# Row statistics of eight output tiles: running sums on ScalarE in place of bn_stats on VectorE, in an attention and spectral kernel

## The chip, the cores and the metric

The kernel runs on one core of one Trainium2 chip. The metric is the device time of one execution in microseconds (us). Before the change three runs gave 3757.16 us in the median (3756.23 to 3763.47). Differences are also given as a share of that.

A core has five engines with queues of their own: TensorE (PE, matmuls; its weight loads are listed as PEld), VectorE (DVE), ScalarE (ACT), GpSimd (POOL) and SyncE (SP, which issues DMA transfers). Each works through its own queue in order; semaphores make one wait for another.

## The reference

Two layers, each an attention block and a two-dimensional spectral filter, both with a layer norm in front and a residual. S is 2048 rows, D is 1024 columns, there are 32 heads of 32.

```python
def _A_ref(x, wqkv, wo):
    qkv = (x @ wqkv).reshape(B, S, 3, H, Dh).transpose(2, 0, 3, 1, 4)
    q, k, v = qkv[0], qkv[1], qkv[2]
    scores = jnp.einsum("bhqd,bhkd->bhqk", q, k) * (Dh ** -0.5)
    o = jnp.einsum("bhqk,bhkd->bhqd", _softmax(scores), v)
    return o.transpose(0, 2, 1, 3).reshape(B, S, D) @ wo

def _B_ref(x, w_r, w_i):
    X = jnp.fft.rfft2(x, axes=(-2, -1)) * (w_r + 1j * w_i)
    return jnp.fft.irfft2(X, s=(S, D), axes=(-2, -1))

for _ in range(2):
    x = x + _A_ref(_layernorm(x), wqkv, wo)
    x = x + _B_ref(_layernorm(x), w_r, w_i)
```

The change lies in the seam between the two: the output projection `@ wo` with its residual, and the mean and variance of every finished row, which the second layer norm needs.

## The kernel before

**Attention.** The heads are taken in 8 groups of four (`g`, 0 to 7). In a group, the queries are taken in 4 chunks of 512 (`c`) and the keys in 16 tiles of 128 (`kt`). One step (c, kt) is called a unit here; two units in a row make a slot, and a group has slots 0 to 31, eight to a chunk. For each unit `S` (line 703) lets TensorE form the scores of four heads in two PSUM tiles `s` from the pool psS, which has three buffers (L709), and ScalarE their exponentials `p` (L713). Every second unit, `PV` (L715) multiplies the last two units' `p` with the values (L719). `add` (L726) lets VectorE add `p` to two running sums `acc` in the tile R (L730, L732); these become the softmax's denominators. At a chunk's end, within the first unit of the next chunk, `fin` (L735) lets TensorE sum `acc` over the keys with a matrix of ones (L739, eight matmuls for four heads, into a psS tile `z`), and VectorE divides (L740 to L746). L739 therefore waits for the chunk's last add.

**The output projection.** It is spread over the loop as filler work for TensorE. A row tile has 128 rows and 1024 columns; tiles are numbered 0 to 15, four to a query chunk. `wo_parts` forms what the first seven head groups give to a tile (L538, with VectorE adding the residual at L564). The last head group's share can only be formed when that chunk's attention is done. So in group 7 `wo_rest(t)` (L598) finishes tile t: six matmuls of a psS tile (`wo_last`, L573, through L538; shown as s<-big,ohl), then L579 on VectorE, which scales, adds and so empties the psS buffer, then two `bn_stats` (L581), a store of the row tile to `y` (L582, from the SP queue) and a `bn_aggr` into `mvs` (L600), which holds mean and variance of tiles 0 to 11. Tiles 0 to 3 belong to chunk 0 and are finished in slots of chunk 1, and so on.

**What sets the order.** TensorE's and ScalarE's queues in the loop are in the order in which the code is written (`manual_schedule`). The table at L763 says in which slot of group 7 each tile is finished, and `share` (L762) how many filler matmuls follow in each slot. VectorE, GpSimd and SP are ordered by the scheduler.

**Behind the loop** `fold_rests` (L610) turns `mvs` into scales on GpSimd and normalises tiles 0 to 11 on ScalarE (L615), while TensorE forms tiles 12 to 15.

Of the kernel before, what the change touches and what calls it, by code (L numbers as in the profile page):

```python
# [6 lines left out]
F32 = mybir.dt.float32  # L7
# [4 lines left out]
AF = mybir.ActivationFunctionType  # L12
ALU = mybir.AluOpType
# [205 lines left out]
def run(g):  # L219
    for _ in g:  # L220
        pass
# [115 lines left out]
def attention(nc, tc, layer, ap, xin, yd, wts, wo, cst, dram, flags):  # L337
# [8 lines left out]
    sq, on, on2, sm = ap.sq, ap.on, ap.on2, ap.sm  # L346
# [14 lines left out]
    V, K, Q, bias, nrm, mx = {}, {}, {}, {}, {}, {}  # L361
# [15 lines left out]
    def turn_x(xn):  # L377
        p = psS.tile([128, 2, 512], F32, name="s").rearrange("p h (d n) -> p (h d) n", n=128)
        for d in range(8):
            nc.tensor.transpose(p[:, d], xn[:, 128 * d:128 * d + 128], cst["ident"])  # L380
        return p
# [107 lines left out]
    def sums(ph):  # L489
        return 8 if ph[0] == "v" else 4  # L490
# [41 lines left out]
    def wo_mm(p, c, t, n, ds, start=True, stop=True):  # L532

        for d in ds:
            oh, ol = ((olast[c][:, i] if d == 7 else osb[c][:, i, d])[:, t * 128:t * 128 + 128] for i in range(2))
            wh, wl = (wo_t[i][d // 4][:, d % 4, n * 512:n * 512 + 512] for i in range(2))
            for i, (a, b) in enumerate(((oh, wh), (oh, wl), (ol, wh))):
                nc.tensor.matmul(p, a, b, start=start and d == ds[0] and i == 0, stop=stop and d == ds[-1] and i == 2)  # L538
                yield
# [10 lines left out]
    mvs = sm.tile([128, 24], F32, name="mvs")  # L550
# [19 lines left out]
                    nc.vector.bn_aggr(mvs[:, 8 * c + 2 * t:8 * c + 2 * t + 2], st)  # L570
            yield

    def wo_last(c, t, p, src, y, start):  # L573

        for n in range(2):
            run(wo_mm(p[:, n], c, t, n, (7,), start=start))
        st = sm.tile([128, 2, 6], F32, name="st")
        r0 = c * 512 + t * 128
        nc.vector.scalar_tensor_tensor(y, p.rearrange("p n c -> p (n c)"), 1.0 / (SO * SW), src, op0=ALU.mult, op1=ALU.add)  # L579
        for n in range(2):  # L580
            nc.vector.bn_stats(st[:, n], y[:, n * 512:n * 512 + 512])  # L581
        nc.sync.dma_start(yd[r0:r0 + 128, :], y)  # L582
        return st

    wo_dst = [ap.x[:, 10 + t if t in SPILL else t] for t in range(8)] + [None] * 2 + [ap.x[:, t] for t in (10, 11)]
# [11 lines left out]

    def wo_rest(t):  # L598
        p = psS.tile([128, 2, 512], F32, name="s")
        nc.vector.bn_aggr(mvs[:, 2 * t:2 * t + 2], wo_last(t // 4, t % 4, p, wo_dst[t], wo_dst[t], True))  # L600

    def scale_bias(mv, n, m):

# [23 lines left out]
    with tc.manual_schedule(engines={mybir.EngineType.PE, mybir.EngineType.DVE, mybir.EngineType.Activation}):  # L627
# [14 lines left out]
        p = turn_x(xn)  # L642
# [13 lines left out]
        p = turn_x(xn)  # L656
# [4 lines left out]
        p = turn_x(xn)  # L661
# [5 lines left out]
        p = turn_x(xn)  # L667
# [35 lines left out]
    def S(g, c, kt):  # L703

        s = [psS.tile([128, 2, 512], F32, name="s") for _ in range(2)]
        for i, (a, b) in enumerate(((0, 0), (0, 1), (1, 0))):
            for h in range(4):
                r = slice(32 * h, 32 * h + 32)
                nc.tensor.matmul(s[h // 2][:, h % 2], K[g][r, a, kt * 128:kt * 128 + 128],  # L709
                                 Q[g][r, b, c * 512:c * 512 + 512], start=i == 0, stop=i == 2)  # L710
        for hf in range(2):
            p = P[g, c, kt, hf] = pp.tile([128, 2, 512], F32, name="p")
            nc.scalar.activation(p, s[hf], AF.Exp, bias=bias[g], scale=SCALE / (SQ * SQ))  # L713

    def PV(g, c, kt):  # L715
        if kt == 0:
            O[g, c] = psO.tile([128, 512], F32, name="o")
        for h in range(4):
            nc.tensor.matmul(O[g, c][32 * h:32 * h + 32], V[g][:, kt, 32 * h:32 * h + 32], P[g, c, kt, h // 2][:, h % 2],  # L719
                             start=kt == 0, stop=kt == NKT - 1)  # L720
        if kt == NKT - 1:
            o = ap.oc.tile([128, 512], F32, name="oc")
            nc.scalar.copy(o, O[g, c])
            O[g, c] = o

    def add(g, c, kt):  # L726
        for hf in range(2):
            p = P[g, c, kt, hf]
            if kt == 1:
                nc.vector.scalar_tensor_tensor(acc[hf], P[g, c, 0, hf], 1e-34, p, op0=ALU.add, op1=ALU.add)  # L730
            elif kt:
                last_add = nc.vector.tensor_add(acc[hf], acc[hf], p)  # L732
        return last_add if kt > 1 else None

    def fin(g, c):  # L735
        zt = on.tile([128, 16, 32], F32, name="zt")
        z = psS.tile([128, 2, 512], F32, name="s")[:, 0]
        for h in range(4):
            nc.tensor.matmul(z[32 * h:32 * h + 32], cst["ones"], acc[h // 2][:, h % 2], start=True, stop=True)  # L739
        nc.vector.transpose(zt.rearrange("p a b -> p (a b)"), z)  # L740
        rc = sm.tile([128, 16], F32, name="rc")
        nc.vector.reciprocal(rc, zt[:, :, 0])
        nc.vector.tensor_max(flags["r"], flags["r"], rc)
        r = on.tile([128, 512], F32, name="zt")
        nc.vector.transpose(r.rearrange("p (a b) -> p a b", b=32), rc.unsqueeze(2).broadcast_to([128, 16, 32]))
        nc.vector.scalar_tensor_tensor(r, O[g, c], SO, r, op0=ALU.mult, op1=ALU.mult)  # L746
        O[g, c] = r
# [12 lines left out]
    fill, lwo, wof = filler(), load_wo(), wo_parts()  # L760
    left, rests = 16, {}
    share = [21] * 10 + [7] * 6 + [11, 10] * 6 + [12] * 4  # L762
    for t, n in zip(range(11), (11, 12, 14, 15, 20, 22, 24, 26, 28, 29, 30)):  # L763
        rests[n] = t

    def slots(f, sums, n, steps):

        while sums:
            k = max(1, int(n / sums + 0.5))
            m = -(-steps // k)  # L770
            for i in range(0, steps, m):
                while ripe():
                    norms()
                for _ in range(min(m, steps - i)):
                    next(f, None)
                n -= 1
                yield sums - (i + m >= steps)
            sums -= 1

    with tc.manual_schedule(engines={mybir.EngineType.PE, mybir.EngineType.Activation}):  # L780
        for g in range(NG):
            todo = sum(sums(ph) for ph in beside.get(g, []))
            sl = slots(fill, todo, 22 if g == NG - 2 else 32, 24)
            wsl = slots(wof, 4, 10, 21)
            for u in range(NCH * NKT):
                c, kt = divmod(u, NKT)
                S(g, c, kt)
                if g == u == 0:
                    run(last_v)
                if kt % 2 == 0:  # L790
                    for w in pend:
                        PV(*w)
                    late = pend
                    pend = []
                    if kt == 0 and late:
                        for w in late:
                            last_add = add(*w)
                        with tc.issue_after(last_add.ins):
                            wts.look()
                        done = [late[1][:2]]  # L800
                        fin(*done[0])
                        late = []
                for w in late[:1]:
                    add(*w)
                late = late[1:]
                if kt == 5 and done:
                    out(*done.pop())
                pend.append((g, c, kt))
                if kt % 2 == 0:
                    continue  # L810
                if todo:
                    todo = next(sl)
                elif g == NG - 2:
                    if left:
                        run(lwo)
                        left = 0
                    if next(wsl, None) is not None and u == NCH * NKT - 1:
                        run(wsl)
                elif g == NG - 1:
                    if u // 2 in rests:  # L820
                        wo_rest(rests[u // 2])
                    for _ in range(share[u // 2]):
                        next(wof)
                if g == NG - 2 and todo <= 6 and left > (8 if todo > 4 else 0):
                    next(lwo)
                    left -= 1
        for w in pend:
            PV(*w)
        for w in late + pend:
            add(*w)  # L830
        run(wof)
    assert not wts.unseen and not wts.cols
    with tc.manual_schedule(engines={mybir.EngineType.PE}):
        ps, xs, folds = [], [xres(3, t) for t in range(4)], fold_rests()

# [557 lines left out]
```

## Time and profile before

| | us |
|---|---|
| median of three runs | 3757.16 |
| lowest, highest | 3756.23, 3763.47 |
| the profiled execution | 3758.82 |
| its span, first to last instruction | 3757.0 |

The profiled execution is a run of its own; its span is what the views cut up. A page of the profile gives busy time by engine, 40 slices, queues, the chain of work that ended last, and the costliest groups of instructions. Views of the trace give one engine's instructions in order of time, each with start, length, engine, line, operation, tile names and, in brackets, the idle time ahead of it and what ended that. Equal instructions in a row are merged, with their count behind an x. A view of stretches gives for each the busy time of every engine and the clock granted to TensorE (1.00 is full). Group 7 of layer 0 runs from about 1310 to 1580 us in the span, that of layer 1 from about 3180 to 3450 us. The costliest groups as the page has them (line, engine, operation, tiles, shapes, count; busy us, mean ns of one; idle time ahead of them and what ended most of it):

```profile
L713 ACT ACTIVATE p<-s,bias 128x1024 f32<-128x1024 f32 x2048 | 2171.5, 1112 | 555.6 <-PE s L709 537.6
L732 DVE TENSOR_TENSOR R<-R,p 128x1024 f32<-128x1024 f32 x1792 | 2088.1, 1218 | 126.1 <-ACT p L713 123.9
L719 PE MATMUL o<-p,R 128*32 128x512 f32 x8192 | 984.9, 598 | 0.0
```

### The profile page before, as it was taken

What the parts mean: (1) busy time and instruction counts of PE and PEld (TensorE: products, weight loads), DVE (VectorE), ACT (ScalarE), POOL (GpSimd) and SP (SyncE); (2) the same over time, 40 slices, a digit from 0 to 9 for tenths busy, and PEclk for the clock granted to TensorE, in tenths of its full rate; (3) what the DMA queues carried; (4) which work ended last, traced back from release to release, by engine and by line L of the source; (5) the groups of instructions that cost most, each with busy time, mean ns of one, the idle gap of its engine ahead of it and who ended that gap; (6) DMA issues with size and microseconds to landing.
All of it is one profiled execution on the core that took longest, in us unless ns stands there. A gap on an engine that the chain in (4) does not pass through costs nothing.

```text
span 3757.0 us, 80258 instructions
## 1 busy us (share of the span) xinstructions
PE 3688.9 (98%) x33271; PEld 1635.1 (44%) x33271; DVE 3212.6 (86%) x3874; ACT 2900.2 (77%) x3587; POOL 297.8 (8%) x388
## 2 busy tenths in 40 slices
PE   8999999999999999999999999999999999999998
PEld 5333433343343333378963334334433433333788
DVE  7799899989999988975658998999899999789745
ACT  5788888888888866658748888888888888666686
POOL 1000000000000000014410000000000000000243
PEclk9999999999999999999999999999999999999999
DMA  6000000000000211233250000001000102121423
GB/s 194 10 18 18 13 12 18 27 7 18 13 27 16 88 54 65 74 146 104 70 158 21 29 29 24 32 24 35 14 29 29 41 18 82 54 71 68 167 87 108
DMA packets 150120, 198.43 MB, mean 53 GB/s; under 512 B 58225, under 2 KB 104049, under 8 KB 148721
## 3 DMA queue, kind: packets, MB, share of 16 engines
q1 hardware_dynamic: 148416, 192.62, 15.9%
q8 instruction: 263, 4.31, 0.5%
q14 instruction: 113, 0.92, 0.1%
q10 hardware_dynamic: 1328, 0.59, 0.1%
HBM read 132.35 MB, written 48.23 MB: 48 GB/s over the span
## 4 chain that ended last, share of the span: by engine, by line


## 5 line engine op out<-in xcount | busy, mean ns | idle before, releaser
L713 ACT ACTIVATE p<-s,bias 128x1024 f32<-128x1024 f32 x2048 | 2171.5, 1112 | 555.6 <-PE s L709 537.6
L732 DVE TENSOR_TENSOR R<-R,p 128x1024 f32<-128x1024 f32 x1792 | 2088.1, 1218 | 126.1 <-ACT p L713 123.9
L719 PE MATMUL o<-p,R 128*32 128x512 f32 x8192 | 984.9, 598 | 0.0
L420 PE MATMUL x<-big,wqk 128*128 128x512 f16 x2880 | 676.4, 380 | 5.0 <-DVE Q L216 1.9
L709 PEld LDWEIGHTS <-R 32*128 32x128 f16 x12288 | 228.3, 92 | 739.7 <-issue 623.6
L420 PEld LDWEIGHTS <-wqk 128*128 128x128 f16 x3072 | 275.9, 98 | 421.7 <-issue 131.7
L719 PEld LDWEIGHTS o<-p,R 128*32 128x32 f32 x8192 | 213.7, 109 | 523.5 <-issue 523.5
L709 PE MATMUL s<-R 32*128 32x512 f16 x6144 | 425.7, 378 | 0.2
L709 PE MATMUL s<-Q,R 32*128 32x512 f16 x6144 | 425.7, 378 | 0.0
L477 PE MATMUL x<-wv,big 128*128 128x256 f16 x2784 | 330.8, 275 | 6.4 <-DVE R L216 4.6
L477 PEld LDWEIGHTS <-big 128*128 128x128 f16 x3072 | 291.5, 98 | 97.2 <-issue 56.1
L538 PE MATMUL x<-big 128*128 128x512 f16 x1050 | 241.3, 380 | 0.0
L460 POOL PARTITION_ALL_REDUCE mall<-mqk x16 | 38.4, 2400 | 2278.7 <-DVE mqk L454 2267.1
L538 PEld LDWEIGHTS <-big 128*128 128x128 f16 x1344 | 126.1, 98 | 172.7 <-issue 29.6
L730 DVE SCALAR_TENSOR_TENSOR R<-p 128x1024 f32<-128x1024 f32 x128 | 150.9, 1218 | 31.5 <-ACT p L713 31.5
L1055 DVE TENSOR_TENSOR H<-G,H 128x512 f16<-128x512 f32 (+1 forms) x68 | 47.0, 691 | 119.8 <-ACT H L1054 119.6
L1000 ACT COPY U<-ps 64x256 f32<-64x256 f32 (+1 forms) x272 | 97.2, 357 | 10.2 <-PE ps L1007 4.9
L740 DVE STREAM_TRANSPOSE zt<-s 128x512 f32<-128x512 f32 x64 | 45.8, 716 | 66.3 <-PE s L739 66.2
L1000 ACT COPY B<-ps 64x256 f32<-64x256 f32 (+1 forms) x272 | 97.2, 357 | 5.4 <-PE ps L1007 1.7
L1007 PE MATMUL ps<-cbi,H 128*128 128x256 f16 (+1 forms) x792 | 98.5, 273 | 1.1 <-DVE H L1055 0.7
L1007 PE MATMUL ps<-cb,big 128*128 128x256 f16 x780 | 96.7, 273 | 0.0
L1007 PEld LDWEIGHTS <-H 128*128 128x128 f16 (+1 forms) x792 | 76.6, 98 | 12.0 <-DVE H L1055 1.9
(443 smaller groups left out, 2975.8 us busy)
## 6 DMA issues: line engine op xcount, KB each, us to landing
wst<-in_wp SPq DMA_DIRECT2D x96, 256.0 KB, 3.0
R<-y SPq DMA_DIRECT2D x32, 512.0 KB, 5.6
w<-in_w SPq DMA_DIRECT2D x60, 256.0 KB, 2.7
od<-ohl SPq DMA_DIRECT2D x56, 256.0 KB, 2.4
big<-od SPq DMA_DIRECT2D x16, 896.0 KB, 5.8
y<-R SPq DMA_DIRECT2D x20, 512.0 KB, 2.6
wst<-in_wo SPq DMA_DIRECT2D x32, 256.0 KB, 2.7
xres<-in_x SPq DMA_DIRECT2D x16, 512.0 KB, 3.4
```

Of the source, the lines that this page charges most:

```text
L420: nc.tensor.matmul(ps, a, b, start=i == 0, stop=i == 23)
L477: nc.tensor.matmul(ps[:, j], x[c][:, d, o:o + 128], w[:, n, d], start=i == 0, stop=i == 23)
L538: nc.tensor.matmul(p, a, b, start=start and d == ds[0] and i == 0, stop=stop and d == ds[-1] and i == 2)
L709: nc.tensor.matmul(s[h // 2][:, h % 2], K[g][r, a, kt * 128:kt * 128 + 128], Q[g][r, b, c * 512:c * 512 + 512], start=i == 0, stop=i == 2)
L713: nc.scalar.activation(p, s[hf], AF.Exp, bias=bias[g], scale=SCALE / (SQ * SQ))
L719: nc.tensor.matmul(O[g, c][32 * h:32 * h + 32], V[g][:, kt, 32 * h:32 * h + 32], P[g, c, kt, h // 2][:, h % 2], start=kt == 0, stop=kt == ...
L730: nc.vector.scalar_tensor_tensor(acc[hf], P[g, c, 0, hf], 1e-34, p, op0=ALU.add, op1=ALU.add)
L732: last_add = nc.vector.tensor_add(acc[hf], acc[hf], p)
L740: nc.vector.transpose(zt.rearrange("p a b -> p (a b)"), z)
L1000: nc.scalar.copy(ov[64 * r:64 * r + 64, a0:a0 + m, x], tl[64 * x:64 * x + 64, :m, r])
L1007: nc.tensor.matmul(out, l, r, start=k == 0, stop=k == len(mm_) - 1)
L1055: nc.vector.tensor_sub(lo, gs, hi)
```

## The change

For tiles 0 to 7, `wo_last` leaves the two `bn_stats` out, and `wo_rest` the `bn_aggr`. In their place two passes over the finished tile are put in a list, `moments`, and from the next slot on one pass is taken from it in every slot, on ScalarE, behind the slot's exponentials: `wo_mean` copies the tile with a scale of 1/1024 and has the copy's running sum written to `mvs` as the mean; GpSimd scales that to the bias -mean/32 (`nm`); `wo_var`, a slot or more later, squares (x - mean)/32 and has that sum written as the variance. The copies themselves go to a scratch tile `y` that nobody reads. Tiles 8 to 10 keep `bn_stats`. In the table of slots, tiles 2 and 3 move from slots 14 and 15 to 13 and 14, so slot 15, the last of chunk 1, finishes no tile. Behind the new functions the new file's lines have numbers higher by 17, and by 20 behind the loop: L732 is L749 there, L713 is L730, L740 is L757.

```diff
-    def wo_last(c, t, p, src, y, start):
+    def wo_last(c, t, p, src, y, start, later=False):
...
-        for n in range(2):
-            nc.vector.bn_stats(st[:, n], y[:, n * 512:n * 512 + 512])
+        if not later:
+            for n in range(2):
+                nc.vector.bn_stats(st[:, n], y[:, n * 512:n * 512 + 512])
         nc.sync.dma_start(yd[r0:r0 + 128, :], y)
...
     def wo_rest(t):
         p = psS.tile([128, 2, 512], F32, name="s")
-        nc.vector.bn_aggr(mvs[:, 2 * t:2 * t + 2], wo_last(t // 4, t % 4, p, wo_dst[t], wo_dst[t], True))
+        st = wo_last(t // 4, t % 4, p, wo_dst[t], wo_dst[t], True, t < 8)
+        if t < 8:
+            moments.extend((wo_mean, t) if i == 0 else (wo_var, t) for i in range(2))
+        else:
+            nc.vector.bn_aggr(mvs[:, 2 * t:2 * t + 2], st)
+
+    moments, minus = [], {}
+
+    def wo_mean(t):
+        nc.scalar.activation(sq.tile([128, 1024], F32, name="y", tag="sq"), wo_dst[t], AF.Copy, scale=1.0 / 1024,
+                             accum_out=mvs[:, 2 * t:2 * t + 1])
+        b = minus[t] = sm.tile([128, 1], F32, name="nm")
+        nc.gpsimd.tensor_scalar(b, mvs[:, 2 * t:2 * t + 1], -1.0 / 32, None, op0=ALU.mult)
+
+    def wo_var(t):
+        nc.scalar.activation(sq.tile([128, 1024], F32, name="y", tag="sq"), wo_dst[t], AF.Square, bias=minus.pop(t),
+                             scale=1.0 / 32, accum_out=mvs[:, 2 * t + 1:2 * t + 2])
...
-    for t, n in zip(range(11), (11, 12, 14, 15, 20, 22, 24, 26, 28, 29, 30)):
+    for t, n in zip(range(11), (11, 12, 13, 14, 20, 22, 24, 26, 28, 29, 30)):
         rests[n] = t
...
                 elif g == NG - 1:
+                    if moments:
+                        f, t = moments.pop(0)
+                        f(t)
                     if u // 2 in rests:
                         wo_rest(rests[u // 2])
```

VectorE's queue before, at the end of chunk 1 of group 7 in layer 0 (from seven adds ahead of tile 2's L579 to the division of chunk 1):

```order
L732 TENSOR_TENSOR R<-R,p 128x1024 x7
L579 SCALAR_TENSOR_TENSOR R<-s,R 128x1024
L732 TENSOR_TENSOR R<-R,p 128x1024
L581 BN_STATS st<-R 128x6 x2
L600 BN_AGGR mvs<-st 128x2
L732 TENSOR_TENSOR R<-R,p 128x1024 x3
L579 SCALAR_TENSOR_TENSOR R<-s,R 128x1024
L564 SCALAR_TENSOR_TENSOR R<-x,xres 128x512
L581 BN_STATS st<-R 128x6 x2
L732 TENSOR_TENSOR R<-R,p 128x1024
L600 BN_AGGR mvs<-st 128x2
L740 STREAM_TRANSPOSE zt<-s 128x512
```

The same queue now, from tile 0's L579 to the same division (L749 is the add, L757 the division's first step):

```order
L579 SCALAR_TENSOR_TENSOR R<-s,R 128x1024
L749 TENSOR_TENSOR R<-R,p 128x1024 x4
L579 SCALAR_TENSOR_TENSOR R<-s,R 128x1024
L564 SCALAR_TENSOR_TENSOR R<-x,xres 128x512
L749 TENSOR_TENSOR R<-R,p 128x1024 x4
L579 SCALAR_TENSOR_TENSOR R<-s,R 128x1024
L749 TENSOR_TENSOR R<-R,p 128x1024 x4
L579 SCALAR_TENSOR_TENSOR R<-s,R 128x1024
L749 TENSOR_TENSOR R<-R,p 128x1024 x4
L564 SCALAR_TENSOR_TENSOR R<-x,xres 128x512
L749 TENSOR_TENSOR R<-R,p 128x1024
L757 STREAM_TRANSPOSE zt<-s 128x512
```

The statistics are gone from the queue, and five adds stand between tile 3's L579 and the division, where one stood.

ScalarE's queue now, from the mean of tile 0 in slot 12 to the mean of tile 2 in slot 16 (L730 is the exponential, L740 the copy of a finished chunk's `o`; before, only L730 and L740 stood here):

```order
L610 ACTIVATE y,mvs<-R 128x1024
L730 ACTIVATE p<-s,bias 128x1024 x4
L616 ACTIVATE y,mvs<-R,nm 128x1024
L730 ACTIVATE p<-s,bias 128x1024 x4
L610 ACTIVATE y,mvs<-R 128x1024
L730 ACTIVATE p<-s,bias 128x1024 x4
L616 ACTIVATE y,mvs<-R,nm 128x1024
L730 ACTIVATE p<-s,bias 128x1024 x2
L740 COPY oc<-o 128x512
L730 ACTIVATE p<-s,bias 128x1024 x2
L610 ACTIVATE y,mvs<-R 128x1024
```

A mean (L610) or a variance (L616) now stands behind every four exponentials, in slots 12 to 19 without a gap, and again in slots 21 to 28. On TensorE the six matmuls of tiles 2 and 3 stand one slot earlier, and nothing else has moved. On SP the stores of tiles 2 and 3 stand ahead of both loads of the next chunk of `od`; before, one load stood ahead of tile 3's store.

More of the change, by code (lines that the diff above doesn't have):

```diff
@@ L831, in attention @@
         run(wof)
-    assert not wts.unseen and not wts.cols
+    assert not wts.unseen and not wts.cols and not moments
     with tc.manual_schedule(engines={mybir.EngineType.PE}):
```

## The prediction

> **What bounds the kernel now.** The page comes first. Its chain of work that ended last is empty for this program, so the bound is read from busy time by stage and then from the timelines.
>
> ```profile
> PE 3688.9 (98%) x33271; PEld 1635.1 (44%) x33271; DVE 3212.6 (86%) x3874; ACT 2900.2 (77%) x3587; POOL 297.8 (8%) x388
> ```
>
> TensorE is busy for 98% of the span. An edit that only lightens VectorE pays where TensorE waits for VectorE and nowhere else. The next view is busy time in stretches of 20 us through the last head group, once for each layer (columns: busy time and count of each engine, granted clock, DMA).
>
> ```profile
> core 0: us, PE busy (x) PEld busy (x) DVE busy (x) ACT busy (x) POOL busy (x), PEclk, DMA share, GB/s
> 1440.00:1460.00 20.00, 20.00 (x184) 6.19 (x181) 19.97 (x24) 15.34 (x16) 0.00 (x0) 1.00 0.14 54
> 1460.00:1480.00 20.00, 17.49 (x137) 5.40 (x130) 18.75 (x25) 11.08 (x11) 0.00 (x0) 1.00 0.52 171
> ...
> 3340.00:3360.00 20.00, 17.49 (x139) 4.58 (x128) 16.73 (x21) 10.80 (x12) 0.00 (x0) 0.91 0.43 142
> ```
>
> The reader is to see 20.00 of 20.00 for TensorE, with VectorE full beside it (19.97), and then one hole of 2.51 us in each layer. The hole lies at the end of chunk 1 (slot 15) of group 7. The waits between 1437 and 1477 us name who was late:
>
> ```profile
> PE s L739 <- DVE R L732: 1.9, 1, 1.9
> ...
> PE s L739 <- DVE R L579: 0.6, 1, 0.6
> ```
>
> L739 is the four column-sum matmuls of `fin`. They wait for the psS buffer that tile 3's L579 empties, then for the last running add (L732). The timeline of TensorE shows the same boundary undisturbed (end of chunk 0) and disturbed (end of chunk 1):
>
> ```profile
> 1418.29 1.92 PE L719 MATMUL o<-p,R 128*32 128x512 f32 x16
> 1420.03 1.04 PE L739 MATMUL s<-R,ones 128*32 128x512 f32 x8
> 1421.00 0.83 PE L709 MATMUL s<-Q,R 32*128 32x512 f16 x12
> ...
> 1470.28 1.93 PE L719 MATMUL o<-p,R 128*32 128x512 f32 x16
> 1472.85 1.05 PE L739 MATMUL s<-R,ones 128*32 128x512 f32 x4 [0.64 <-DVE R L579]
> 1475.77 1.05 PE L739 MATMUL s<-R,ones 128*32 128x512 f32 x4 [1.86 <-DVE R L732]
> 1476.75 0.82 PE L709 MATMUL s<-Q,R 32*128 32x512 f16 x12
> ```
>
> From the start of PV (L719) to the next scores (L709) it takes 1421.00 - 1418.29 = 2.71 us undisturbed and 1476.75 - 1470.28 = 6.47 us here. The hole costs 3.76 us, more than its 2.50 us of idleness, because the column sums run in two halves instead of one.
>
> ```profile
> 3339.40 1.92 PE L719 MATMUL o<-p,R 128*32 128x512 f32 x16
> 3341.97 1.05 PE L739 MATMUL s<-R,ones 128*32 128x512 f32 x4 [0.64 <-DVE R L579]
> 3344.88 1.92 PE L739 MATMUL s<-R,ones 128*32 128x512 f32 x4 [1.87 <-DVE R L732]
> 3346.73 1.47 PE L709 MATMUL s<-Q,R 32*128 32x512 f16 x12
> ```
>
> In layer 1 the same stretch takes 3346.73 - 3339.40 = 7.33 us, and the scores behind it take 1.47 instead of 0.83. The excess is 7.33 - 2.71 + 0.64 = 5.26 us. The additional 1.50 us is the clock:
>
> ```profile
> 1474.00:1476.00 2.00, 0.23 (x2) 0.14 (x4) 1.83 (x3) 0.00 (x0) 0.00 (x0) 1.00 0.96 281
> ...
> 3344.00:3346.00 2.00, 1.12 (x4) 0.18 (x4) 0.95 (x2) 0.00 (x0) 0.00 (x0) 0.68 0.96 242
> 3346.00:3348.00 2.00, 2.00 (x14) 0.30 (x12) 1.08 (x4) 0.00 (x0) 0.00 (x0) 0.50 0.96 345
> ```
>
> The granted clock fell to 0.50 behind layer 1's hole and stayed at 1.00 through layer 0's, though both are equally long. In all, the two holes cost 3.76 + 5.26 = 9.02 us of this execution, and that is the most the change can return.
>
> **Part 1, the statistics leave VectorE.**
>
> ```profile
> 1466.78 1.27 DVE L581 BATCH_NORM_STATS2 st<-R 128x6 f32<-128x512 f32 x2
> 1468.09 0.21 DVE L600 BATCH_NORM_AGGREGATE mvs<-st 128x2 f32<-128x12 f32 x1
> 1468.22 3.44 DVE L732 TENSOR_TENSOR R<-R,p 128x1024 f32<-128x1024 f32 x3
> 1471.58 1.22 DVE L579 SCALAR_TENSOR_TENSOR R<-s,R 128x1024 f32<-128x1024 f32 x1
> 1472.71 0.68 DVE L564 SCALAR_TENSOR_TENSOR R<-x,xres 128x512 f32<-128x512 f32 x1
> 1473.31 1.28 DVE L581 BATCH_NORM_STATS2 st<-R 128x6 f32<-128x512 f32 x2
> 1474.50 1.21 DVE L732 TENSOR_TENSOR R<-R,p 128x1024 f32<-128x1024 f32 x1
> ```
>
> One tile's statistics hold VectorE from 1466.78 to 1468.22, or 1.44 us. Four tiles lie in chunk 1; the last has only its two L581 ahead of the last add (1474.50 - 1473.31 = 1.19). So 3 x 1.44 + 1.19 = 5.5 us leave the queue ahead of that add, and it is late by less. The same saving for tiles 4 to 7 in chunks 2 and 3 is worth nothing: TensorE has no hole there.
>
> **Part 2, tiles 2 and 3 come one slot earlier.** Tile 3's matmuls leave slot 15, so L579 no longer holds the psS buffer at the boundary, which is the wait of 0.64. TensorE's total work in the chunk is unchanged, so the column sums become due at the same time, 1470.28 + 1.74 = 1472.02 (1.74 is 1420.03 - 1418.29). But slot 15 is shorter by tile 3's six matmuls, and so its second unit starts later:
>
> ```profile
> 1464.00 1.92 PE L719 MATMUL o<-p,R 128*32 128x512 f32 x16
> 1465.85 0.83 PE L709 MATMUL s<-Q,R 32*128 32x512 f16 x12
> 1466.61 1.47 PE L538 MATMUL s<-big,ohl 128*128 128x512 f16 x6
> 1467.92 1.67 PE L538 MATMUL x<-big 128*128 128x512 f16 x7
> ...
> 1466.71 2.12 ACT L713 ACTIVATE p<-s,bias 128x1024 f32<-128x1024 f32 x2 [0.49 <-PE s L709]
> ```
>
> Six matmuls hold TensorE for 1467.92 - 1466.61 = 1.31, so the scores of that unit move from 1465.85 to 1467.16. The exponential starts 0.86 later (1466.71 - 1465.85) and half of it is done 1.11 later, at 1469.13. VectorE then does one add (1.13), L564 (0.60) and the last add (1.21): 1472.1. VectorE stays the last to arrive, but by 0.1 to 0.2 us instead of 3.7. **Gain**: 9.02 - 2 x 0.15 = 8.7 us.
>
> On the SP queue, tile 2's and 3's stores are issued a slot earlier and both loads of the next `od` chunk stand behind them. That chunk is first read behind the loop, by the matmuls of tiles 12 to 15, so I cost it at nothing.
>
> **Part 3, sixteen new passes a layer on ScalarE.** No row shows an ACTIVATE with a running sum, so its parts are bounded:
>
> ```profile
> L215 ACT ACTIVATE hl<-xn 128x1024 f16<-128x1024 f32 x24 | 25.2, 1051 | 0.4
> L615 ACT ACTIVATE xn<-R,b,r 128x1024 f32<-128x1024 f32 x20 | 23.3, 1230 | 9.9 <-POOL b L607 9.9
> L1000 ACT COPY U<-ps 64x128 f32<-64x128 f32 x24 | 6.3, 261 | 0.5
> ```
>
> L215 is the same copy with a fixed scale, 1.05 us; L615 has two operands per partition, 1.23; Square with one lies between, 1.14. Let e be what the sum itself adds. It is 0 at the least and 0.26 if reading the sum out is one short pass of its own (L1000); 1.05, the elements gone over twice, is a rival below. I take 0.2, near the short pass; from 0 to 0.26 the sum moves by 0.5 us. What must hide the passes is ScalarE's idle time ahead of the next exponential:
>
> ```profile
> 1464.10 2.12 ACT L713 ACTIVATE p<-s,bias 128x1024 f32<-128x1024 f32 x2 [1.55 <-PE s L709]
> ...
> 1486.49 2.12 ACT L713 ACTIVATE p<-s,bias 128x1024 f32<-128x1024 f32 x2 [0.90 <-PE s L709]
> ...
> 1488.24 0.83 PE L709 MATMUL s<-Q,R 32*128 32x512 f16 x12
> ```
>
> In a slot of chunk 1 with a tile there are 1.55 us. In a slot without a tile (chunks 2 and 3) there are 0.90, and a further 0.6 until TensorE needs the buffer, since the first half at 1486.49 ends at 1487.60 and the scores that reuse it start at 1488.24. Room 1.5 us stands against a pass of 1.0 + e (passes overlap by 0.1), so the cover holds up to e = 0.5. The wait on L579 is met: a tile's mean comes one slot behind the tile. GpSimd's `nm` has a whole slot between the two passes.
>
> One place is tight. Tile 1's variance stands in slot 15, ahead of chunk 2's first exponential. The pass starts at about 1470.1 and ends at 1471.2 + e, the exponential's second half at 1473.35 + e, and the scores behind the column sums want that buffer at 1473.3. That costs 0.1 + e = 0.3 us a layer. **Sum**: 8.7 - 2 x 0.3 = 8.1 us off.
>
> **The clock rule.** The trace shows a half clock behind one of two equal holes. The Trainium skill, TensorE: Matmul & The Clock Gate, section "What's actually happening", says that the gate halves the clock after an idle window of about 3.4 us, that the window runs free, and that its place therefore varies from run to run. By that rule runs of before pay this 1.5 us for none, one or both holes, and the sum would be 6.6, 8.1 or 9.6 us; one dip in two holes agrees with it, and no run here shows how often it falls.
>
> The sum is made against the profiled execution: 3758.82 - 8.1 = 3750.7. The median of the runs, 3757.16, lies 1.66 lower, about one dip. From the median it is 3749.1 with a dip in it and 3757.16 - 6.6 = 3750.6 without. I forecast **3750.0**.
>
> **Rivals.** 0.2% of this kernel, 7.5 us, is about what a measurement can tell from no change, and the forecast lies close to it; so the sign is surer than the verdict.
> - *The hole only shrinks* (0.17). VectorE remains last at the boundary, so each 0.5 us that a semaphore or a later add costs there comes back, and the two halves could split again for up to 1 us. For it: the margin is negative by my own count. Against: 3.7 us shrink to 0.15. It gives 8.1 - 2 x 1.2 = 5.7, or 3751 to 3753.
> - *ScalarE becomes the bound, slower than before* (0.10). Where e exceeds 0.5, each pass in a slot without a tile delays the scores by e - 0.5: slots 16 to 19, 21, 23, 25 and 27, eight a layer. At e = 1.05 the cost is 16 x 0.55 = 8.8, plus 2 x 1.15 at the boundary, against 8.7: about 3759.6 to 3761. It decides from e = 0.9 on, a pass of 2.0 us. For it: no row shows the sum. Against: that would be a second pass over the tile. The Trainium skill, ScalarE: Activation LUTs, section "Rules for kernel authors", speaks on this side: adds and multiplies belong on VectorE, not ScalarE; per tile 2.2 us of passes do replace 1.44 here, but on the engine that is idle.
> - *A dip in both holes of ordinary runs* (0.18). 9.6 off, 3747 to 3748.
> - *Nothing is gained* (0.08). The hole moves to chunk 2's end, where the trace has none now and VectorE has less to do: 3756 to 3758.
>
> The forecast itself has 0.47 (3748.5 to 3751.5). Over 0.2% faster is below 3749.65: the dip in both holes, 0.18, and four tenths of the forecast's own case, 0.19, together 0.37. Over 0.2% slower needs e of about 1.35 or an unseen wait, 0.06 of the slower rival's 0.10. The rest, 0.57, is within 0.2%. The range, 3746.5 to 3756.5, takes in all but the slower rival and half of the last.
>
> **What would show it.** Right: TensorE busy 20.00 of 20.00 at the end of chunk 1 in both layers, the column sums as eight in one row, no L739 waiting for L579, the granted clock at 1.00 there, a mean pass of 1.1 to 1.3 us, and TensorE never waiting for ScalarE at L709. Wrong: a wait of L739 on L732 above half a microsecond, passes near 2 us, or scores held up in slots 16 to 27. The forecast falls if the passes are long, or if ordinary runs of before do not have these holes.

## The result, and the profile after

| | before | after |
|---|---|---|
| median, us (13 runs each) | 3757.99 | 3750.78 |
| lowest, highest | 3754.81, 3763.47 | 3748.47, 3753.37 |
| span of the profiled execution | 3757.0 | 3748.0 |
| ratio, 95% interval | | 0.9981 (0.9972 to 0.9989) |

The change takes 0.19% off, 7.2 us between the medians. The forecast was 3750.0.

The page of the profile after begins with the busy time of each engine:

```profile
PE 3685.4 (98%) x33271; PEld 1635.9 (44%) x33271; DVE 3195.4 (85%) x3826; ACT 2932.8 (78%) x3651; POOL 304.3 (8%) x404
```

VectorE has 48 instructions fewer (16 tiles with two `bn_stats` and a `bn_aggr`), ScalarE 64 more, and not 32: each pass is two instructions. The same stretches as before, now without a hole (columns as before):

```profile
1460.00:1480.00 20.00, 20.00 (x179) 6.49 (x176) 17.61 (x19) 17.49 (x21) 1.12 (x2) 1.00 0.44 156
...
3340.00:3360.00 20.00, 20.00 (x180) 6.31 (x182) 18.44 (x18) 18.71 (x23) 1.26 (x2) 1.00 0.08 33
```

TensorE's timeline at the end of chunk 1 in layer 0 (L736 is PV, L756 the column sums, L726 the scores):

```profile
1469.63 1.92 PE L736 MATMUL o<-p,R 128*32 128x512 f32 x16
1471.37 1.20 PE L756 MATMUL s<-R,ones 128*32 128x512 f32 x8
1472.51 0.98 PE L726 MATMUL s<-Q,R 32*128 32x512 f16 x12
```

The column sums are eight in one row again. From PV to the scores it takes 1472.51 - 1469.63 = 2.88 us instead of 6.47; undisturbed it is 2.71. Two small remainders are to be seen: the column sums take 1.20 instead of 1.04, and the scores 0.98 instead of 0.83. VectorE's timeline at the same place shows the first one's cause:

```profile
1468.51 1.23 DVE L749 TENSOR_TENSOR R<-R,p 128x1024 f32<-128x1024 f32 x1 [0.25 <-ACT p L730]
1469.65 0.68 DVE L564 SCALAR_TENSOR_TENSOR R<-x,xres 128x512 f32<-128x512 f32 x1
1470.25 1.22 DVE L749 TENSOR_TENSOR R<-R,p 128x1024 f32<-128x1024 f32 x1
```

The last add ends at 1471.47, one tenth of a microsecond behind the start of the column sums; the second four of the eight, which read its sum, are still held up a little. VectorE now waits for ScalarE (0.25) where before it ran without a break.

**A measure that repeats.** The time of a whole execution scatters by 0.1 to 0.2% from lowest to highest. The stretch from chunk 0's column sums to the first matmul behind the loop does not, but for dips of the granted clock, and the edits of this study act in it. Its two ends, of before and of after, in layer 0:

```profile
1420.03 1.04 PE L739 MATMUL s<-R,ones 128*32 128x512 f32 x8
...
1579.25 9.24 PE L538 MATMUL s<-big 128*128 128x512 f16 x42
```

```profile
1419.38 1.04 PE L756 MATMUL s<-R,ones 128*32 128x512 f32 x8
...
1575.17 9.24 PE L538 MATMUL s<-big 128*128 128x512 f16 x42
```

That is 159.22 and 155.79 us. In layer 1 the ends are 3289.15 and 3449.88 before, 3284.48 and 3440.27 after: 160.73 and 155.79. So the two layers give 3.43 + 4.94 = 8.37 us of the 9.0 by which the profiled spans differ; the other 0.6 lies outside, where the scatter is larger than that. The first long wait of TensorE behind the loop (4.88 us) ends 47.6 us behind the loop's end in both. All runs by this measure:

| run | layer 0 | layer 1 | time of the run or median, us |
|---|---|---|---|
| before | 159.22 | 160.73 | 3757.99 |
| before, second profile | 159.23 | 159.22 | 3754.28 (one run) |
| before, third profile | 159.21 | 159.22 | 3752.60 (one run) |
| after | 155.79 | 155.79 | 3750.78 |
| after, second profile | 155.79 | 155.78 | 3751.51 |
| table alone | 159.42 | 159.43 | 3755.72 |
| statistics alone | 155.94 | 155.95 | 3750.77 |
| no passes on ScalarE | 155.63 | 155.63 | 3749.65 (one run) |
| passes twice | 163.50 | 163.51 | 3763.03 (one run) |
| passes for tiles 0 to 3 alone | 155.78 | 155.79 | 3752.12 (one run) |
| filler in elevens and tens, VectorE unchanged | 155.47 | 155.47 | 3749.74 |

One more run, with the filler at 18 and 12, is told of below; its slots divide the work differently, so this stretch doesn't compare.

### The profile page after: what moved, and what is told of

It is laid out like the page before. It is cut to its first block, busy times and chain, and to the rows that moved or that the text cites. A ratio compares the mean times of both kernels' runs of the same rounds, so it can differ in the third digit from the quotient of the medians.

```text
span 3748.0 us, 80321 instructions
## 1 busy us (share of the span) xinstructions
PE 3685.4 (98%) x33271; PEld 1635.9 (44%) x33271; DVE 3195.4 (85%) x3826; ACT 2932.8 (78%) x3651; POOL 304.3 (8%) x404
## 4 chain that ended last, share of the span: by engine, by line
## 5 line engine op out<-in xcount | busy, mean ns | idle before, releaser
L730 ACT ACTIVATE p<-s,bias 128x1024 f32<-128x1024 f32 x2048 | 2171.5, 1112 | 515.0 <-PE s L726 496.3
L749 DVE TENSOR_TENSOR R<-R,p 128x1024 f32<-128x1024 f32 x1792 | 2090.6, 1220 | 137.3 <-ACT p L730 134.1
L736 PE MATMUL o<-p,R 128*32 128x512 f32 x8192 | 985.0, 598 | 0.0
L726 PEld LDWEIGHTS <-R 32*128 32x128 f16 x12288 | 228.5, 92 | 739.2 <-issue 623.1
L736 PEld LDWEIGHTS o<-p,R 128*32 128x32 f32 x8192 | 213.7, 109 | 523.4 <-issue 523.4
L726 PE MATMUL s<-R 32*128 32x512 f16 x6144 | 425.9, 378 | 0.5 <-ACT p L730 0.3
L726 PE MATMUL s<-Q,R 32*128 32x512 f16 x6144 | 425.3, 377 | 0.0
L757 DVE STREAM_TRANSPOSE zt<-s 128x512 f32<-128x512 f32 x64 | 45.8, 716 | 65.7 <-PE s L756 65.6
```

## The experiments

Theory A is that of the prediction: TensorE sets the time, and the only thing in the way is VectorE's lateness at the end of chunk 1. Rival B gives the gain to the new slots of tiles 2 and 3, rival C to a lighter VectorE, or a fuller ScalarE, throughout the group.

**The table alone.**

```diff
-    for t, n in zip(range(11), (11, 12, 14, 15, 20, 22, 24, 26, 28, 29, 30)):
+    for t, n in zip(range(11), (11, 12, 13, 14, 20, 22, 24, 26, 28, 29, 30)):
```

> The kernel before with only the new table of slots (tiles 2 and 3 in slots 13 and 14); all statistics stay on VectorE. Measure: time from the column sums of chunk 0 to the first matmul behind the loop of group 7, 159.22 us (layer 0) and 160.73 us (layer 1) before, 155.79 in both after. Theory A (the hole is VectorE's lateness at the end of chunk 1, and the statistics are the load): VectorE has the same work ahead of the last add, so nothing is gained; 159.2 in layer 0, a hole of 2.5 to 3.9 us at or just ahead of the column sums, time within 2 us of before. Rival B (tile 3's psS buffer held the boundary, so the table does the work): about 156.4, the hole gone, some 6 us less per execution.

Measured: 159.42 and 159.43 us, a ratio of 0.9997 (0.9987 to 1.0006). TensorE's timeline of this run, its four waits at the end of chunk 1:

```profile
1460.78 0.83 PE L709 MATMUL s<-Q,R 32*128 32x512 f16 x12 [0.31 <-DVE R L579]
...
1467.84 0.83 PE L709 MATMUL s<-Q,R 32*128 32x512 f16 x12 [0.71 <-DVE R L579]
...
1473.86 1.05 PE L739 MATMUL s<-R,ones 128*32 128x512 f32 x4 [0.96 <-DVE R L732]
1475.50 1.05 PE L739 MATMUL s<-R,ones 128*32 128x512 f32 x4 [0.59 <-DVE R L732]
```

The idle time is nearly the same as before, 0.31 + 0.71 + 0.96 + 0.59 = 2.57 us against 2.50, but cut into four. VectorE is as late as it was; tiles finished earlier only make TensorE wait earlier. Rival B falls.

**The statistics alone**: the change with the old table.

```diff
-    for t, n in zip(range(11), (11, 12, 13, 14, 20, 22, 24, 26, 28, 29, 30)):
+    for t, n in zip(range(11), (11, 12, 14, 15, 20, 22, 24, 26, 28, 29, 30)):
```

> The change without its table: tiles 0 to 7 take their statistics on ScalarE, tiles 2 and 3 stay in slots 14 and 15. Theory A: nearly the whole gain, 155.9 us from the column sums of chunk 0 to the end of the loop in both layers (155.79 with the table), since 5.5 us leave VectorE and slot 15 is longer again; time as after. Rival B: most of the hole stays, 158 to 159 us, because L579 of tile 3 still empties the psS buffer late.

Measured: 155.94 and 155.95 us, 0.9984 (0.9975 to 0.9994). TensorE's timeline has one short wait, now for ScalarE, and an undisturbed boundary:

```profile
1460.63 1.45 PE L538 MATMUL s<-big,ohl 128*128 128x512 f16 x6 [0.19 <-ACT p L730]
...
1472.31 1.04 PE L756 MATMUL s<-R,ones 128*32 128x512 f32 x8
1473.29 0.83 PE L726 MATMUL s<-Q,R 32*128 32x512 f16 x12
```

The statistics carry the gain; the table adds 0.15 us a layer to it. Without the statistics VectorE empties the psS buffer of tile 3 in time even in slot 15. The wait of 0.19 comes from a variance pass in slot 13, which has no tile under the old table. The column sums take 1.04 here and 1.20 in after, so what is left of the hole there comes with the new table: it removes the delay behind slot 13 and brings back a smaller one at the boundary.

**No passes on ScalarE.** Mean and variance of tiles 0 to 7 are left out; `mvs` is filled with a constant 1.0 in their place.

```diff
+    nc.gpsimd.memset(mvs, 1.0)
...
-            moments.extend((wo_mean, t) if i == 0 else (wo_var, t) for i in range(2))
+            pass
```

> The change with neither the statistics of tiles 0 to 7 on VectorE nor the passes on ScalarE: mean and variance of these tiles are left out (a constant 1.0 stands in mvs). What the passes cost is the difference to after. Theory A (the passes lie in ScalarE's idle time, all but 0.1 to 0.2 us at the boundary): 155.6 us from chunk 0's column sums to the end of the loop, the scores behind chunk 1's column sums take 0.83 and not 0.98. Rival C (the passes do delay the exponentials and so TensorE throughout): 153 to 154.5 us.

Measured: 155.63 us in both layers, 0.16 less than after.

```profile
1471.19 1.20 PE L757 MATMUL s<-R,ones 128*32 128x512 f32 x8
1472.32 0.83 PE L727 MATMUL s<-Q,R 32*128 32x512 f16 x12
```

The scores behind the column sums take 0.83 again, so the 0.98 of after is the pass in slot 15, and the passes cost no more than that by the stretch. The column sums still take 1.20: that remainder is VectorE's, under the new table.

**Each pass twice in a row.**

```diff
-        nc.scalar.activation(sq.tile(...), wo_dst[t], AF.Copy, scale=1.0 / 1024, accum_out=...)
+        for _ in range(2):
+            nc.scalar.activation(sq.tile(...), wo_dst[t], AF.Copy, scale=1.0 / 1024, accum_out=...)
```

and the same for the square (arguments shortened here).

> The change with every pass on ScalarE made twice in a row (same results). It puts the price and the point of the slower rival to the test: room for a pass in a slot without a tile is 1.5 us, and two passes need 2.2 to 2.4. Theory A: TensorE now waits for the exponentials at L709's place in slots 16 to 19, 21, 23, 25 and 27, 0.7 to 0.9 us each, and up to 1.2 us behind chunk 1's column sums: 161 to 163 us in each layer, 10 to 14 us more per execution than after, so slower than before. Rival C' (ScalarE has more room than I counted, since it is busy for only 78% of the span): below 157.5 us.

Measured: 163.50 and 163.51 us, 7.7 a layer more than after and a little above what was expected; one run of 3763.03 us. ScalarE's timeline in slot 15, and behind it TensorE's:

```profile
1471.40 1.15 ACT L619 ACTIVATE y<-R,nm 128x1024 f32<-128x1024 f32 x1
1472.45 0.20 ACT L619 ACTIVATION_READ_ACCUMULATOR y<-R,nm 128x1 f32 x1
1472.68 1.15 ACT L619 ACTIVATE y<-R,nm 128x1024 f32<-128x1024 f32 x1
1473.74 0.19 ACT L619 ACTIVATION_READ_ACCUMULATOR y<-R,nm 128x1 f32 x1
1473.83 2.10 ACT L733 ACTIVATE p<-s,bias 128x1024 f32<-128x1024 f32 x2
```

```profile
1474.97 0.39 PE L729 MATMUL s<-Q,R 32*128 32x512 f16 x2 [0.33 <-ACT p L733]
1475.98 0.82 PE L729 MATMUL s<-Q,R 32*128 32x512 f16 x10 [0.61 <-ACT p L733]
...
1488.44 0.82 PE L729 MATMUL s<-Q,R 32*128 32x512 f16 x10 [0.40 <-ACT p L733]
```

The exponentials come late and the scores wait for their buffers: the slower rival's mechanism. The view of waits lists nine at the scores in this stretch, 3.3 us together: two at the boundary, and seven behind seven of the eight slots that the prediction named. Each of the seven is shorter (0.23 to 0.51) than was expected (0.7 to 0.9). Four waits of 0.18 at tiles' matmuls were not expected; the view's 4.0 us are little more than half of the 7.7. The engine's share of the whole span (78% busy in after) says nothing of it; the room is counted slot by slot.

**Passes for tiles 0 to 3 alone**; tiles 4 to 7 keep `bn_stats`.

```diff
-        if t < 8:
+        if t < 4:
```

(the same bound in the call of `wo_last`)

> The change with the passes on ScalarE for tiles 0 to 3 only; tiles 4 to 7 keep bn_stats on VectorE. Theory A: the second half of the conversion is worth nothing, as chunks 2 and 3 have no hole: 155.8 us from the column sums of chunk 0 to the end of the loop in both layers, as after (155.79). Rival C (a lighter VectorE helps all along): half the gain, 157 to 157.6 us.

Measured: 155.78 and 155.79 us, as after. The second half of the conversion is worth nothing, and costs nothing. Rival C falls on both sides.

**VectorE's work unchanged, the filler moved.** If the hole is only VectorE's lateness, time given to VectorE in chunk 1 must fill it as well. The first attempt:

```diff
-    share = [21] * 10 + [7] * 6 + [11, 10] * 6 + [12] * 4
+    share = [18] * 10 + [12] * 6 + [11, 10] * 6 + [12] * 4
```

> The kernel before with one other edit and no pass on ScalarE: the filler matmuls of group 7 are spread more evenly, 18 a slot in slots 0 to 9 and 12 in slots 10 to 15, in place of 21 and 7 (252 in both). TensorE then gives VectorE 1.1 us more in each of slots 10 to 15, 6.6 us against the 5.5 us of statistics. Theory A (the hole is VectorE's lateness in chunk 1 and nothing else): the hole goes without any change to VectorE's work. From the first column sums of group 7 to the end of its loop it took 267.96 us before (layer 0) and 264.53 after; here 264.2, column sums as eight in one row, and a ratio to before of 0.998, as after or 0.3 us better in each layer. Rival: the hole moves into slots 0 to 9 or to chunk 0's end, where TensorE now gives less time; above 266 us.

Measured: 3794.17 us, 1.0097 (1.0081 to 1.0114). TensorE's timeline of this run, and VectorE's at the same place:

```profile
1363.88 0.82 PE L538 MATMUL x<-big 128*128 128x512 f16 x3
1367.01 5.08 PE L538 MATMUL x<-big 128*128 128x512 f16 x15 [2.31 <-DVE R L564]
```

```profile
1366.27 0.68 DVE L564 SCALAR_TENSOR_TENSOR R<-x,xres 128x512 f32<-128x512 f32 x1
```

A half tile has 21 matmuls, and psX, the one PSUM buffer in which the filler forms them, holds one half tile. With 18 a slot a half ends in mid-slot; the next one must wait until VectorE reaches L564 behind its adds. The view of waits for layer 0's group 7 has ten of them, 19.6 us in all and 3.0 the longest:

```profile
PE x L538 <- DVE R L564: 19.6, 10, 3.0
```

My expectation had missed this buffer, so the run says nothing about theory A. It does show the clock behind unbroken waits. Around the wait of 2.31 us the stretches read (third from the end is the granted clock):

```profile
1364.00:1367.00 3.00, 0.70 (x3) 0.20 (x2) 2.75 (x4) 2.10 (x2) 0.00 (x0) 1.00 0.00 0
1367.00:1368.00 1.00, 0.99 (x3) 0.34 (x3) 1.00 (x1) 0.00 (x0) 0.00 (x0) 0.64 0.00 0
1368.00:1370.00 2.00, 2.00 (x6) 0.76 (x5) 0.08 (x1) 0.00 (x0) 0.00 (x0) 0.50 0.00 0
```

Of the twenty waits in the two layers' groups, the six of 2.31 to 2.98 us were followed by a half clock four times, the fourteen of 0.85 to 2.15 us never. The second attempt keeps every end of a half at the end of a slot:

```diff
-    share = [21] * 10 + [7] * 6 + [11, 10] * 6 + [12] * 4
+    share = [21] * 8 + [11, 10] * 10 + [12] * 4
```

> The kernel before with one other edit and no pass on ScalarE, built after the first spread of the filler (18 and 12 a slot) had cost 36 us: there a half tile (21 matmuls into the one psX buffer) ended in the middle of a slot, and TensorE stood still until VectorE's L564 had emptied the buffer. Here each half ends at a slot's end: 21 a slot in slots 0 to 7, then 11 and 10 in turn to slot 27 (426 in all, as before). Slots 8 to 15 give VectorE 21 matmuls, 4.6 us, more behind slot 9 than they did. Theory A: the hole goes with VectorE's work unchanged; 155.4 to 155.6 us from chunk 0's column sums to the end of the loop in both layers (159.22 before, 155.79 after), no wait of TensorE for L564, and a time like that of after run beside it. Rival B (only taking the statistics off VectorE removes the hole): above 157 us.

> The changed kernel once more, beside the run ahead of it on the same chip: 155.79 us from chunk 0's column sums to the end of the loop in both layers, a ratio to before of 0.998, and no more than 0.05% from the run with the filler spread.

Measured on the same chip: 3749.74 us, 0.9977 (0.9968 to 0.9986), with the filler moved; 3751.51, 0.9984 (0.9975 to 0.9993), with the change. The times can't be told apart; the stretch can, 155.47 against 155.79.

```profile
1471.06 1.92 PE L719 MATMUL o<-p,R 128*32 128x512 f32 x16
1472.80 1.04 PE L739 MATMUL s<-R,ones 128*32 128x512 f32 x8
1473.77 0.82 PE L709 MATMUL s<-Q,R 32*128 32x512 f16 x12
```

The boundary takes 1473.77 - 1471.06 = 2.71 us, undisturbed, with all `bn_stats` on VectorE. That one line replaces the whole change, and is 0.32 us a layer better by the stretch. It does not give chunk 1 more filler: slots 8 to 15 have 84 of these matmuls in both kernels. Before, VectorE stood idle early in the chunk, in slots 8 and 9:

```profile
1428.41 2.36 DVE L732 TENSOR_TENSOR R<-R,p 128x1024 f32<-128x1024 f32 x2 [1.21 <-ACT p L713]
...
1434.52 0.69 DVE L564 SCALAR_TENSOR_TENSOR R<-x,xres 128x512 f32<-128x512 f32 x1 [1.13 <-PE x L538]
1436.42 2.36 DVE L732 TENSOR_TENSOR R<-R,p 128x1024 f32<-128x1024 f32 x2 [1.21 <-ACT p L713]
```

With three smaller waits that is 4.59 us of idleness between the chunk's first adds and 1441; with the filler moved it is 1.24. The 5.5 us of statistics made VectorE late because its slots from 10 on were short, not because the chunk as a whole had no room.

**Before, profiled twice more**, for the clock behind the holes.

> The kernel before, profiled once more, for the clock behind its two holes. By the reading of one dip in two holes as chance: each hole is followed by a half clock or not, 159.2 or 160.7 us from chunk 0's column sums to the end of the loop, layer by layer, and not always in layer 1. If the dip belongs to layer 1: 159.2 and 160.7 again.

> As the run ahead of it, a third profile of the kernel before: 159.2 or 160.7 us in each layer.

Measured: 159.23, 159.22, 159.21 and 159.22 us; all four holes without the half clock. The stretch of layer 1 in the first of them:

```profile
3342.00:3344.00 2.00, 1.38 (x12) 0.37 (x16) 0.96 (x3) 0.00 (x0) 0.00 (x0) 1.00 0.90 272
3344.00:3346.00 2.00, 2.00 (x17) 0.79 (x9) 1.83 (x5) 1.53 (x2) 0.00 (x0) 1.00 1.06 403
```

The granted clock, third from the end, stays at 1.00 through the end of layer 1's hole and behind it, where the first profile of before had the half clock. So the dip does not come with every hole of layer 1. It fell behind one of six equal holes.

## Why the prediction was right

- **The bound and the place**: right. The two holes were costed at 3.76 and 5.26 us; 3.43 and 4.94 came back.
- **Part 1**: right. What counts is the statistics of tiles 0 to 3 ahead of chunk 1's last add; those of tiles 4 to 7 are worth nothing (155.78 with and without).
- **Part 2**: right at the boundary, wrong in what it credits to the table. That VectorE would stay last by 0.1 to 0.2 us is what the timeline shows (0.17 at the column sums). But the wait of 0.64 for tile 3's buffer was credited to the new table, and goes with the statistics alone (no wait for it in that run, with the old table); the table is worth 0.15 us a layer.
- **Part 3**: e, what the running sum adds to a pass, was taken as 0.2. The trace has it as an instruction of its own, and the pass itself is hardly slower than its nearest rows. The groups of the mean's and the variance's line (count, then least, median and most ns), and ScalarE's timeline in slot 15:

```profile
L610 ACT ACTIVATE y<-R x16: 1054/1057/1069, 1450.5 to 3410.1; 128x1024 f32<-128x1024 f32 x16
L610 ACT ACTIVATION_READ_ACCUMULATOR y<-R x16: 193/198/203, 1451.5 to 3411.1; 128x1 f32 x16
...
L616 ACT ACTIVATE y<-R,nm x16: 1145/1148/1157, 1456.9 to 3415.7; 128x1024 f32<-128x1024 f32 x16
```

```profile
1469.37 1.15 ACT L616 ACTIVATE y<-R,nm 128x1024 f32<-128x1024 f32 x1
1470.41 0.20 ACT L616 ACTIVATION_READ_ACCUMULATOR y<-R,nm 128x1 f32 x1
1470.50 2.11 ACT L730 ACTIVATE p<-s,bias 128x1024 f32<-128x1024 f32 x2
```

  The read overlaps by 0.1 with the pass ahead of it and by 0.1 with the exponential behind it. So this variance pass holds ScalarE for 1470.50 - 1469.37 = 1.13 us, where two passes in a row without a read would take 1.148 less the overlap of 0.1, or 1.05. So e was 0.1, half of what was taken, and a mean costs some 1.05 by the same sum (an estimate). The tight place in slot 15 was put at 0.3 us a layer and is 0.16.
- **The sum**: 8.1 us against the profiled execution, which has one dip of the clock; by the stretch it is 8.4.
- **The clock rule** (the Trainium skill, TensorE: Matmul & The Clock Gate, section "What's actually happening"): with a dip in one of six holes the runs agree that it comes and goes with the run. They do not bear out a whole idle window of 3.4 us as its condition: the longest unbroken wait in a hole is 1.86 us, and with the filler at 18 and 12 four dips stood behind unbroken waits of 2.31 to 2.98. What decides when it comes is not shown. The median then holds 2 x 3.43 = 6.9 us and, at 1.5 us in one of six, 0.5 on average: 7.4, against 7.2 measured. The forecast from the median without a dip was the nearer one, but the interval of the ratio, 4.1 to 10.5 us in time, holds them all, so the medians cannot decide between these sums. That 3750.0 came within 0.8 us of the measured median is partly luck.
- **The rivals**: the hole shrank to 0.17 us, not to 1. The slower rival is real as a mechanism, but needs a pass twice as long. The Trainium skill, ScalarE: Activation LUTs, section "Rules for kernel authors", would keep the additions on VectorE; here the passes take longer than what they replace (some 2.2 us a tile against 1.44) and still pay, though a better spread of TensorE's filler pays as much and leaves them on VectorE.

What was not tried: the change and the moved filler together, and other tables of slots.

## What to carry to other kernels

Where one engine is busy all along, look for the stretch in which it is not, and count what a second engine has to do ahead of the one wait that ends there: here 5.5 us of work that stood in front of an add, and both ways tried of getting that add done earlier were worth nearly the same. Before moving work to another engine, look whether the late engine stood idle a little earlier, and try giving it that time at the late place by moving the filler of the busy one, and keep the filler's units whole where a single buffer stands between them. Room on the engine that takes the work is counted from its idle time in front of each urgent instruction, not from its share of the span.

## What the runs showed of the hardware

A running sum on ScalarE is a second instruction of 0.19 to 0.20 us, of which 0.1 is left after its overlaps; the pass it belongs to takes 1.057 us against 1.051 without one. Six equal idle stretches of TensorE, in all 2.5 us each with four narrow matmuls between the parts, were followed by a half clock once. Unbroken waits of 2.31 to 2.98 us (filler at 18 and 12) were followed by one in four of six cases, those of up to 2.15 us in none of fourteen. Cut into four waits (the table alone), the same idle time was not followed by one in either layer. The stretch of 155 to 160 us in group 7 repeats to 0.02 us from run to run where no dip falls into it, while the 1700 us between the two layers' stretches took 1706.2 to 1709.9 us in three profiles of one kernel.
